# Three edits to a linear-attention and feed-forward kernel: the last tile's stores, one whole tile's store, and the grouping of batch 1's key-value products

## Chip, core and metric

The kernel runs on one core of a Trainium2 chip. The metric is the device time of one execution in microseconds; the time before is the median of three runs. All times in this document are microseconds unless marked ns.

## What is computed

The inputs are float32. Attention has no softmax: for each of 8 batches and 8 heads, with 576 positions of width 64, k and v are contracted over the positions into a 64 x 64 matrix, q is multiplied by it, and each row is divided by its root mean square and scaled. Heads are joined to rows of 512, 4608 rows in all, which go through a feed-forward layer of width 2048 with a gated activation.

```python
kv = np.einsum('bhsd,bhse->bhde', k, v)
out = np.einsum('bhsd,bhde->bhse', q, kv)
rms = np.sqrt(np.mean(out * out, axis=-1, keepdims=True) + 1e-06)
x = out / rms * g_norm                       # to (4608, 512)
h = x @ w_in                                 # (512, 2048)
g = h * (1.0 / (1.0 + np.exp(-1.702 * h)))
return (g @ w_out).astype(np.float32)        # (2048, 512)
```

## The kernel before

**Tiles.** The 4608 rows are nine tiles of 512. Tiles 0 to 7 hold 512 of the 576 positions of batches 0 to 7; tile 8 (t == B) holds the 64 positions left over of each of the eight batches. For each tile, `layers` (L758) runs the first layer (`hid_seven`, or `first_columns` for tile 0) and the second layer (`Seven.run`, L671, or `project_all`, L787, for tile 0). From tile 1 on both layers work on half-size blocks with seven products in place of eight. The attention of batch t + 1 is done in between the matmuls of tile t.

**Order of the work.** The schedule is manual: instructions stand on each engine's queue in the order in which the program makes them. `at1(i, ...)` and `at2(i, ...)` (L963, L966) put a unit of attention work behind step i of the first or second layer of the tile. Each engine takes its queue in order and waits where data is missing; SP, ACT and POOL each have a queue of DMAs besides.

**Tile 0's second layer** (`project_all`) has 64 steps, each one matmul of 128 x 512 (L795) into one of four row blocks `mo`. The steps go four output-weight blocks `fo` at a time for each `mo`; the steps from 48 on take blocks 12 and 13, then those from 52 on blocks 14 and 15. The output weights come in six loads by POOL (`load_w_out`, L195), interleaved with the loads of batch 1's q, k and v (`early_load`, L89; k and v in two halves, chunks 0 and 1, then 2 and 3). The last of these loads is that of blocks 14 and 15 (L907).

Batch 1's attention stands among these steps (L988 to L994), by chunks c of two heads: `kv(c)` (L226) makes twelve small matmuls (`early_kv_product`, L246, matmul at L250) of 96 rows and 64 columns for chunk c. After the second chunk of a pair `keep_kv` (L384) copies the pair's result to the block-diagonal weights `kvb` with two DVE copies (L387). `out(c)` (L283) multiplies q by them and squares the result on ACT (L301), `ss(c)` (L358) sums the squares with a matmul of ones and takes the root on ACT (L360), and `apply(c)` (L372) multiplies on DVE into the next tile's rows. `load_kv` (L111, POOL) for batch 2 overwrites the buffers of k and v, in two parts at steps 39 and 51; the second has DVE mask the rest rows first (`clear_rest`, L124).

**Stores.** A tile's output is gathered in `osb` (two buffers, taken in turn). `Seven.run` makes the output in quarters (i, j): i the upper or lower half of the row blocks, j the left or right half of the columns. `ORDER` (L592) makes products 1, 5, 6, 2, 7, 3, 4; `LAST` (L593), for tile 8, has 3 ahead of 7. `place` (L650) puts a quarter into `osb`: product 2 ends (0, 0), 3 ends (0, 1), 7 ends (1, 1) and 4 ends (1, 0). Every product has two halves of eight matmuls, one for each of two row blocks `mo`; in tile 8 the quarters of products 7 and 4 are placed by halves, as soon as one is done.

For tiles in `HALVED` (L953) `place` stores the upper half of the rows after quarter (0, 1) and the lower half after (1, 0), 512 KB each, on SP (`store`, L825). The other tiles from 2 to 7 are stored whole, 1 MB, behind the second layer (L774).

Tile 8 is stored by `store_rest(mo, n0, n1)` (L704): the columns n0 to n1 of one row block, which holds 64 rows of each of two batches, in two DMAs. Block 0 goes out on POOL, the others on SP and ACT, one DMA each. Blocks 0 and 1 go out at quarter (0, 1), with all 512 columns; block 3's right half at the end of (1, 1); block 2 at the first half of (1, 0); block 3's left half at the second.

Of the kernel before, what the change touches and what calls it, by code (L numbers as in the profile page):

```python
# [16 lines left out]
def kernel(  # L17
# [13 lines left out]
    DM = H * D  # L31
# [45 lines left out]
    HF, HN = FO // 2, DM // 2  # L77
# [430 lines left out]
    def copy(engine, to, src):  # L508
        (nc.vector.tensor_copy if engine == "D" else nc.scalar.copy)(to, src)  # L509
# [79 lines left out]
    class Seven:  # L589
# [60 lines left out]
        def place(self, name, mo, with_, i, j):  # L650
            ps, m = self.ready(name, mo)
            if ps is None:
                return
            o = osbs[self.t][:, 2 * i + m.start : 2 * i + m.stop, j * HN : (j + 1) * HN]
            if with_:
                nc.vector.tensor_add(o, ps, self.kept[with_][:, m])  # L656
            else:
                copy = nc.vector.tensor_copy if self.t == B else nc.scalar.copy
                copy(o, ps)
            if self.t == B:  # L660
                if (i, j) == (0, 1):
                    store_rest(0, 0, DM)
                    store_rest(1, 0, DM)
                elif i == 1 and mo == 0 and j == 0:
                    store_rest(2, 0, DM)
                elif i == 1 and mo == 1:
                    store_rest(3, j * HN, (j + 1) * HN)
            elif self.t in HALVED and j == 1 - i:
                store(self.t, 2 * i, 2 * i + 2)
# [34 lines left out]
    def store_rest(mo, n0, n1):  # L704
        osb = osbs[B]
        for g in range(2):
            rows = out[(2 * mo + g) * S : (2 * mo + g + 1) * S, n0:n1]
            if 2 * mo + g < EARLY:
                p0 = SM % PE_
                rows = rows[bass.DynSlice(NJ * p0 + SM // PE_, R, step=NJ), :]  # L710
            else:
                rows = rows[SM:S, :]
            queue = nc.gpsimd if mo == 0 else (nc.sync, nc.scalar)[g]
            queue.dma_start(out=rows, in_=osb[g * R : (g + 1) * R, mo, n0:n1])  # L714
# [43 lines left out]
    def layers(t, units1, units2):  # L758
        hid = d0 if t == 0 else Hidden(t)
        seven = Seven(t, hid.gT) if t else None  # L760
        left = hid_seven(t, hid, seven, units1) if t else first_columns(hid, units1)
        osbs[t] = opool.tile([P, 4, DM], F32, name="osb", tag="osb")
        if t:
            todo = {n: [lambda x=x: seven.sums(*x) for x in xs] for n, xs in plan(t).later.items()}
            for n, us in units2.items():
                todo.setdefault(n, []).extend(us)
            for n, us in left.items():
                todo[n] = us + todo.get(n, [])
            seven.run(todo)
        else:  # L770
            project_all(hid.gT, units2)
        if t < EARLY:
            store_early(t)
        elif t < B and t not in HALVED:  # L774
            store(t, 0, J)
# [38 lines left out]
    def store_early(t):  # L814
        n = 0
        while n < SM:
            mo, j, p = n // P, n // PE_, n % PE_
            m = min((mo + 1) * P, (j + 1) * PE_) - n
            nc.sync.dma_start(
                out=out[t * S : (t + 1) * S, :][bass.DynSlice(NJ * p + j, m, step=NJ), :],  # L820
                in_=osbs[t][n % P : n % P + m, mo, :],
            )
            n += m

    def store(t, j0, j1):  # L825
        nc.sync.dma_start(
            out=out[t * S : t * S + SM, :].rearrange("(p j) m -> p j m", j=J)[:, j0:j1],
            in_=osbs[t][:, j0:j1],
        )
# [120 lines left out]
    def plan(t):  # L950
        return SECOND if t < EARLY else LATER if t < B - 1 else LAST_TWO

    HALVED = (2, 3, 4, 5, 6)  # L953
    live = {0: a0}

    def start(b):
# [2 lines left out]
    for t in range(NT):  # L959
        b = t + 1  # L960
        u1, u2 = {}, {}

        def at1(i, f, *args):  # L963
            u1.setdefault(i, []).append(lambda: f(*args))

        def at2(i, f, *args):  # L966
            u2.setdefault(i, []).append(lambda: f(*args))  # L967

        def of(b, name, *args):
            return lambda: getattr(live[b], name)(*args)  # L970

        if t == 0:
            for l in range(2):
                at1(6, nc.vector.memset, kvd[l], 0.0)
            at1(7, of(0, "out", NPAIR))
            at1(7, scale_w_in, 0, 4)
            at1(7, w_in_sums, 0, 2)
            at1(8, start, 1)
            at1(12, scale_w_in, 4, 6)
            at1(12, w_in_sums, 2, 3)  # L980
            at1(13, load_q, 2)
            at2(4, setattr, a0, "ss_pool", Attention.ss_pool)
            at2(4, of(0, "ss", NPAIR, True))
            at2(4, of(0, "apply", NPAIR))
            at2(18, weight_sum, 0, 0, HF)
            at2(18, scale_w_in, 6, 8)
            at2(18, w_in_sums, 3, 4)
            for c in range(NPAIR):  # L988
                at1(12, of(1, "pack_q", c))
                at2(9 + 3 * c, of(1, "q", c))  # L990
                at2((36, 37, 49, 50)[c], of(1, "kv", c))
                at2((41, 43, 54, 55)[c], of(1, "out", c))
                at2((45, 50, 58, 60)[c], of(1, "ss", c))
                at2((48, 52, 58, 62)[c], of(1, "apply", c))  # L994
            for n in range(1, 4):
                at2(19, weight_sum, n, 0, 4)
                at2(38, weight_sum, n, 4, 6)
            at2(39, load_kv, 2, 0, H // 2, False)
            at2(51, clear_rest)
            at2(51, load_kv, 2, H // 2, H)  # L1000

            def first_sum():
                made[1] = Sums(1, xT[1])
                made[1].form(0)

            at2(55, first_sum)
        elif b < B:
            todo = plan(t)
            at1(todo.steps.index("kv"), of(b, "kv_all", todo.keep))
            if t == 1:  # L1010
                at1(5, start, b)
                at1(5, of(b, "transpose_q"))
                at1(4, nc.scalar.preload_act_table_set, "gelu_apprx_sigmoid_and_others")
                for n, i in ((1, 8), (2, 11), (3, 16)):
                    at1(i, weight_sum, n, 6, HF)
            if t + 2 < B:
                late = max(15, todo.steps.index("kv") + 1)
                at1(late, load_kv, t + 2)
                at1(late, load_q, t + 2)
                at2(100, start, t + 2)  # L1020
                at2(100, of(t + 2, "transpose_q"))
            at = todo.attn
            at2(at["table"], nc.scalar.preload_act_table_set, "abs_reciprocal_sqrt_and_small")
            for h in range(2):
                at2(at["roots"][h], of(b, "roots", h))
            for j in range(J):
                if j < J // 2:
                    at2(at["rows"][j], of(b, "rows", j))
                for name in ("add_up", "turn"):
                    at2(at[name][j], of(b, name, j))  # L1030
            at2(46, of(b, "out", NPAIR))
            at2(74, of(b, "ss", NPAIR))
            at2(80, of(b, "apply", NPAIR))
            at2(82, nc.scalar.preload_act_table_set, "gelu_apprx_sigmoid_and_others")
        elif t < B:
            for name in ("ss_pool", "rest_pool"):
                at2(16, setattr, live[1], name, (ps_a, "att"))
            at2(16, of(1, "out", NPAIR))
            at2(34, nc.scalar.preload_act_table_set, "abs_reciprocal_sqrt_and_small")
            at2(44, of(1, "ss", NPAIR))  # L1040
            at2(50, of(1, "apply", NPAIR))
            at2(52, nc.scalar.preload_act_table_set, "gelu_apprx_sigmoid_and_others")
        layers(t, u1, u2)
# [30 lines left out]
```

## Time and profile before

| | |
|---|---|
| median of three runs | 260.13 |
| range of the three | 260.03 to 260.14 |
| the profiled execution, its own time | 260.59 |
| its span | 258.8 |
| TensorE busy | 251.4 (97%) |
| VectorE busy | 195.1 (75%) |
| ScalarE busy | 174.9 (68%) |
| bytes moved by DMA | 35.33 MB |

The span runs from the first to the last recorded instruction; the time of an execution is longer by what lies around it, here 1.8. In the views PE is TensorE, PEld its weight loads, DVE VectorE, ACT ScalarE, POOL GpSimd and SP SyncE; a "q" behind the name marks an engine's sequencer, where DMAs are issued. L250 is line 250 of the kernel.

The page's strips cut the span into 40 slices of 6.5; a digit is the busy share in tenths. The chain that ended last is followed back from the last instruction, at each step to what released it; its rows hold start, length, and what. A row of a timeline holds start, length from the first start to the last end, engine, line, operation, tiles (out<-in), shape and count; in brackets stands the engine's idle time ahead of it and what ended it. Matmuls are pipelined: one's length is longer than the distance to the next start. A row of DMA issues holds tiles, queue, count, size of one, and the time from issue to landing. A row of windows holds the window, its length, and for each engine its busy time and count, then the granted clock, the DMA engines' busy share and their GB/s.

### The profile page before, as it was taken

How to read it: one execution, taken by the hardware profiler on the slowest of the kernel's cores; microseconds unless marked ns; L12 is line 12 of the kernel's file. 1: busy time of each engine (PE TensorE's matmuls, PEld its weight loads, DVE VectorE, ACT ScalarE, POOL GpSimd, SP SyncE). 2: the span in 40 equal slices, each digit the busy share in tenths (PEclk: the TensorE clock that was granted, in tenths of full speed). 3: DMA queues.
4: the chain of work that ended last, by engine and by line, in shares of the span. 5: the costliest groups of instructions: out<-in, count | busy, mean ns of one | idle time of the engine just before them, and what ended most of it. 6: DMA issues, size and time to landing. Idle time of an engine off the chain costs nothing.

```text
span 258.8 us, 6349 instructions
## 1 busy us (share of the span) xinstructions
PE 251.4 (97%) x2596; PEld 203.7 (79%) x2596; DVE 195.1 (75%) x351; ACT 174.9 (68%) x315; POOL 53.8 (21%) x81
## 2 busy tenths in 40 slices
PE   8889999999999999999999999999999999999993
PEld 2434454788888888888888888888888888888882
DVE  1565685899968896899689968996899687557842
ACT  3378734988749974997489748984798569737820
POOL 8773245107026001600170007000000000000001
PEclk9999999999999999999999999999999999999999
DMA  7999999999989957996799579947600610021005
GB/s 169 192 196 205 205 204 197 218 214 124 175 182 150 226 66 154 159 214 79 167 152 221 65 177 149 228 50 178 160 4 0 172 73 3 0 89 77 3 0 162
DMA packets 68559, 35.33 MB, mean 136 GB/s; under 512 B 37874, under 2 KB 65778, under 8 KB 68402
## 3 DMA queue, kind: packets, MB, share of 16 engines
q0 software_dynamic: 37520, 18.17, 54.4%
q1 hardware_dynamic: 30688, 16.36, 26.9%
q8 instruction: 20, 0.33, 0.5%
q10 hardware_dynamic: 322, 0.39, 0.4%
q14 instruction: 9, 0.07, 0.1%
HBM read 36.70 MB, written 9.44 MB: 178 GB/s over the span
## 4 chain that ended last, share of the span: by engine, by line
PE 92%; DMA 4%; DVE 1%; issue 0%; ACT 0%; POOL 0%
PE o L681 38%; PE h L559 38%; PE o L795 6%; PE hT L452 5%; DMA qraw<-in_q_dram 2%; DMA vbuf<-in_v_dram 2%; PE kvp L238 2%; PE outR L313 1%; PE ss L358 1%; PE kvp L250 0%; PE outT L283 0%; PE q L433 0%; DVE xT L368 0%; PE outT L287 0%; ACT rs L360 0%
## 5 line engine op out<-in xcount | busy, mean ns | idle before, releaser
L539 ACT ACTIVATE gT<-h 128x512 f16<-128x512 f32 x96 | 52.5, 602 | 5.4 <-PE h L559 5.4
L559 PEld LDWEIGHTS <-ws 128*128 128x128 f16 x512 | 50.1, 98 | 5.8
L681 PEld LDWEIGHTS <-gS 128*128 128x128 f16 x512 | 49.4, 98 | 6.2 <-DVE gS L611 0.3
L559 PE MATMUL h<-xS,ws 128*128 128x256 f16 x384 | 52.2, 273 | 0.0
L681 PE MATMUL o<-tw,gS 128*128 128x256 f16 x384 | 46.5, 273 | 0.0
L681 PEld LDWEIGHTS <-gT 128*128 128x128 f16 x384 | 37.6, 98 | 4.3
L559 PEld LDWEIGHTS <-w_in_sb 128*128 128x128 f16 x384 | 37.1, 98 | 4.7
L559 PE MATMUL h<-xT,w_in_sb 128*128 128x256 f16 x224 | 31.9, 273 | 0.0
L681 PE MATMUL o<-w_out_sb,gT 128*128 128x256 f16 x256 | 31.4, 273 | 0.0
L573 DVE TENSOR_TENSOR h<-h,s 128x512 f32<-128x512 f32 x32 | 22.2, 698 | 6.8 <-PE h L559 5.5
L575 DVE TENSOR_TENSOR s<-h,s 128x512 f32<-128x512 f32 x32 | 22.1, 692 | 4.1 <-PE h L559 3.3
L656 DVE TENSOR_TENSOR osb<-o,qf 128x512 f32<-128x512 f32 (+1 forms) x25 | 16.7, 668 | 11.2 <-PE o L681 8.3
L114 POOL DMA_DIRECT2D kraw<-in_k_dram x7 | 6.0, 853 | 90.6 <-PE kvp L238 86.4
L611 DVE TENSOR_TENSOR gS<-gT 128x512 f16<-128x512 f16 (+2 forms) x32 | 21.3, 686 | 0.6 <-ACT gT L539 0.6
L539 ACT ACTIVATE gT<-s 128x512 f16<-128x512 f32 x32 | 19.8, 628 | 2.6 <-DVE s L575 2.6
L714 POOL DMA_DIRECT2D out_dram<-osb x2 | 1.1, 562 | 92.0 <-DVE osb L656 92.0
L559 PE MATMUL h<-xS,w_in_sb 128*128 128x256 f16 x128 | 18.9, 273 | 0.0
L360 ACT ACTIVATE rs<-ss,eps_t 128x512 f32<-128x512 f32 (+1 forms) x16 | 9.2, 581 | 13.8 <-PE ss L358 13.7
L967 ACT ACT_TABLE_LOAD x14 | 18.0, 1283 | 0.2
L648 ACT COPY qf<-o 128x512 f32<-128x512 f32 (+1 forms) x26 | 14.2, 547 | 4.5 <-PE o L681 4.3
L329 DVE TENSOR_REDUCE sum<-sq 128x8 f32<-128x512 f16 x24 | 15.3, 678 | 2.5 <-ACT sq L323 2.5
L509 ACT COPY h<-h 128x512 f32<-128x512 f32 x27 | 15.7, 586 | 2.1 <-PE h L559 2.0
(100 smaller groups left out, 362.9 us busy)
## 6 DMA issues: line engine op xcount, KB each, us to landing
out_dram<-osb SPq DMA_DIRECT2D x10, 512.0 KB, 3.6
kraw<-in_k_dram POOLq DMA_DIRECT2D x5, 512.0 KB, 9.2
vbuf<-in_v_dram POOLq DMA_DIRECT2D x5, 512.0 KB, 12.1
qraw<-in_q_dram POOLq DMA_DIRECT2D x3, 512.0 KB, 13.2
qbuf<-in_q_dram POOLq DMA_DIRECT2D x3, 512.0 KB, 13.4
out_dram<-osb SPq DMA_DIRECT2D x6, 192.0 KB, 6.2
w_in_sb<-in_moe_w_in_dram POOLq DMA_DIRECT2D x2, 512.0 KB, 10.7
w_out_sb<-in_moe_w_out_dram POOLq DMA_DIRECT2D x2, 512.0 KB, 15.3
```

The source lines that it names most:

```text
L329: nc.vector.tensor_reduce(out=self.sum4[:, j, :], in_=self.o[j][1].rearrange("p (x d) -> p x d", d=D), op=ALU.add, axis=mybir.AxisListType.X,)
L509: (nc.vector.tensor_copy if engine == "D" else nc.scalar.copy)(to, src)
L539: nc.scalar.activation(self.gT[:, to, n * TH : (n + 1) * TH], src, AFT.Gelu_apprx_sigmoid)
L559: nc.tensor.matmul(bank[name][:, a], w, x, start=(p in (1, 5) and a == 0 and k == 0), stop=(k == KH - 1), skip_group_check=True,)
L573: nc.vector.tensor_add(bank["z"], bank["x"], self.s5)
L575: nc.vector.tensor_add(self.s5, bank["x"], self.s5)
L611: op(s[:, n, lo], a, b)
L648: nc.scalar.copy(self.kept[as_][:, m], ps)
L656: nc.vector.tensor_add(o, ps, self.kept[with_][:, m])
L681: nc.tensor.matmul(o, a, w, start=(p in (1, 2, 5) and i == 0 and (mo == 0 or split)), stop=(i == HF - 1), skip_group_check=True,)
L795: nc.tensor.matmul(os[mo], gT[:, fo, mo * P : (mo + 1) * P], w_out_sb[:, fo, :], start=(fo == 0), stop=(fo == FO - 1),)
L967: u2.setdefault(i, []).append(lambda: f(*args))
```

## The change

Three edits. When a quarter of tile 8's upper half is placed, its columns of blocks 0 and 1 are stored: (0, 0) with columns 0 to 255, (0, 1) with 256 to 511. So eight DMAs of 64 KB stand where four of 128 KB stood, half of them at the earlier quarter. Tile 6 leaves `HALVED` and is stored whole, in one DMA behind its second layer. And batch 1's `kv(1)` moves from step 37 to 36, `kv(3)` from step 50 to 49, so that 24 small matmuls follow each other at both places. Within a step, units go in the order in which the loop over c adds them: behind step 50 the `ss(1)` stays, which had stood ahead of `kv(3)` and now comes after it.

```diff
             if self.t == B:
-                if (i, j) == (0, 1):
-                    store_rest(0, 0, DM)
-                    store_rest(1, 0, DM)
+                if i == 0:
+                    for m in range(2):
+                        store_rest(m, j * HN, (j + 1) * HN)
                 elif i == 1 and mo == 0 and j == 0:
                     store_rest(2, 0, DM)
...
-    HALVED = (2, 3, 4, 5, 6)
+    HALVED = (2, 3, 4, 5)
...
-                at2((36, 37, 49, 50)[c], of(1, "kv", c))
+                at2((36, 36, 49, 49)[c], of(1, "kv", c))
```

On each engine's queue this gives: on TensorE the two groups, with nothing else moved; on POOL two more DMAs, on SP one more for tile 8 and one fewer for tile 6, on ACT one more. DVE's and ACT's operations keep their order.

## Prediction

> **What bounds the kernel now.** I read the page first, for the span and the state of the DMA engines, then the chain that ended last.
>
> ```profile
> span 258.8 us, 6349 instructions
> DMA  7999999999989957996799579947600610021005
> PE 92%; DMA 4%; DVE 1%; issue 0%; ACT 0%; POOL 0%
> ```
> ```profile
> 7.95 5.73 DMA vbuf<-in_v_dram
> 13.68 0.14 issue
> 13.81 0.38 PE kv L250 x12
> ...
> 244.02 10.60 PE o L681 x97
> ...
> 254.64 0.42 DVE osb L659
> ```
>
> TensorE carries 92% of the chain, so time taken out of its stream counts, unless something else then comes last. Two stretches are not TensorE's. In the first 45 us the DMA engines are 90% busy or more in nearly every slice; they are loading weights and the inputs of batches 0, 1 and 2. The row of 13.68 shows a landing that TensorE waits for: 0.14 us from landing to first product. The other stretch is the end. The chain closes with a DVE copy at 254.64 + 0.42 = 255.06, but the span lasts to 258.8: 3.7 us in which only stores run. The change touches both stretches, and one quiet place between them.
>
> **Part 1: batch 1's key-value products in two groups of 24.** TensorE's timeline in tile 0's second layer:
>
> ```profile
> 38.48 0.38 PE L250 MATMUL kvp<-vbuf,kraw 96*64 96x64 f16 x12
> 38.79 0.39 PE L795 MATMUL o<-w_out_sb,gT 128*128 128x512 f16 x1
> 39.11 0.38 PE L250 MATMUL kvp<-vbuf,kraw 96*64 96x64 f16 x12
> 39.42 1.04 PE L795 MATMUL o<-w_out_sb,gT 128*128 128x512 f16 x4
> 40.29 0.38 PE L283 MATMUL outT<-qT,kvb 128*128 128x512 f16 x1
> ...
> 42.76 0.38 PE L250 MATMUL kvp<-vbuf,kraw 96*64 96x64 f16 x12
> 43.07 0.39 PE L795 MATMUL o<-w_out_sb,gT 128*128 128x512 f16 x1
> 43.30 0.38 PE L358 MATMUL ss<-sq,ones 128*128 128x512 f16 x1
> 43.60 0.38 PE L250 MATMUL kvp<-vbuf,kraw 96*64 96x64 f16 x12
> 43.91 1.04 PE L795 MATMUL o<-w_out_sb,gT 128*128 128x512 f16 x4
> ```
>
> Matmuls overlap, so I go by starts. Four L795 take 40.29 - 39.42 = 0.87, or 0.22 each. The single one between two key-value groups takes 39.11 - 38.79 = 0.32, so entering a group costs 0.10. Twelve products take 38.79 - 38.48 = 0.31. What 24 take isn't in the trace; the nearest row is a later tile's group of 40:
>
> ```profile
> 57.06 0.82 PE L238 MATMUL kvp<-vbuf,kraw 128*64 128x64 f16 x40
> 57.81 0.61 PE L559 MATMUL h<-xT,w_in_sb 128*128 128x256 f16 x4
> ```
>
> Forty take 0.75, so one more product costs (0.75 - 0.31) / 28 = 0.016, and 24 take 0.31 + 12 x 0.016 = 0.50 where two groups took 0.62. A merge saves 0.12 + 0.10 = 0.22, and both 0.44. That is the upper bound.
>
> The groups and steps also wait for loads, all on POOL's queue: the third and fourth product for the second half of batch 1's v (issued at 30.57), and step 52 of the layer, the first to use output-weight blocks 14 and 15, for the last weight load (issued at 33.10). These are the issues, and for each the size and the time to landing:
>
> ```profile
> 30.57 0.68 POOL L90 DMA_DIRECT2D vbuf<-in_v_dram  x1 [1.91 <-DMA qraw<-in_q_dram]
> 33.10 0.70 POOL L196 DMA_DIRECT2D w_out_sb<-in_moe_w_out_dram  x1 [1.85 <-DMA w_out_sb<-in_moe_w_out_dram]
> ```
> ```profile
> vbuf<-in_v_dram POOLq DMA_DIRECT2D x1, 288.0 KB, 12.0
> ```
> ```profile
> w_out_sb<-in_moe_w_out_dram POOLq DMA_DIRECT2D x1, 256.0 KB, 10.7
> ```
>
> They land at 42.57 and 43.80. Nothing ahead of them in the queue is changed, so they land then after the change too. With the 0.14 of the first fence, the third product can't start before 42.71 and step 52 not before 43.94. The first merge would bring the third product from 42.76 to 42.54: the load holds it at 42.71. From there 24 products (0.50), step 50, the sum of squares, and step 51 (0.22 each) bring step 52 to 43.87: the weights hold it at 43.94. In the trace it starts at 43.91 + 0.22 = 44.13. So 0.19 us is left of 0.44, and what is late next is the weight load. Below, the part is bounded by 0 (the step might be at its load already); I take **0.2**.
>
> The copies of the products to the weights of the next step cost nothing:
>
> ```profile
> 39.53 0.59 DVE L387 CAST kvb<-kvp 64x128 f16<-64x128 f32 x2 [0.70 <-PE kvp L250]
> ```
>
> They begin 0.11 behind the start of the step that follows the group. After the change that step starts at 38.48 + 0.50 = 38.98, the copies end at 39.68, and the product that reads them comes five steps on, at 40.08; the slack grows from 0.17 to 0.40. In the second group it is six matmuls instead of four. The sum of squares of chunk 1 now stands behind the fourth product, at 43.43 instead of 43.30, and its apply is due three steps later, behind the mask of the rest rows on DVE, which itself comes earlier. POOL's loads for batch 2, which wait for these products, are issued up to 0.4 earlier, behind the weights in the same queue.
>
> **Part 2: tile 6 in one transfer.** SP issues the second half of the tile's store at 206.12, and that half takes 2.6 us to land; the whole now goes out at that point:
>
> ```profile
> 206.12 0.33 SPq L826 DMA_DIRECT2D out_dram<-osb  x1
> ```
> ```profile
> out_dram<-osb SPq DMA_DIRECT2D x1, 512.0 KB, 2.6
> ```
>
> At twice the half's time it lands at 211.3. Nothing stands behind it on SP before tile 7's own store, tile 8 first writes the same buffer at 249.46 (fence of part 3), and the DMA engines have little to do in those slices (the page's row). Cost and gain: 0. If that cover were gone, the wait would be for one half more, 2.6.
>
> **Part 3: the last tile's upper left quarter.** DVE makes the upper left quarter at 249.46 and the upper right one at 251.22; the stores of both follow at 251.94 on SP and ACT, at 252.21 on POOL:
>
> ```profile
> 249.46 0.69 DVE L656 TENSOR_TENSOR osb<-o,qf 128x512 f32<-128x512 f32 x1 [2.63 <-issue]
> 251.22 1.23 DVE L656 TENSOR_TENSOR osb<-o,qf 128x512 f32<-128x512 f32 x2 [1.07 <-PE o L681]
> ...
> 251.94 3.62 SPq L714 DMA_DIRECT2D out_dram<-osb  x4
> 252.21 1.11 POOL L714 DMA_DIRECT2D out_dram<-osb  x2 [91.99 <-DVE osb L656]
> ```
>
> What the DMA engines do in each microsecond behind that (the last two columns are their busy share and GB/s), and the size and time to landing of the last two transfers:
>
> ```profile
> 252.00:253.00 1.00, 1.00 (x11) 0.90 (x10) 0.53 (x2) 0.00 (x0) 0.80 (x2) 1.00 0.00 0
> 253.00:254.00 1.00, 1.00 (x11) 0.90 (x10) 0.55 (x2) 0.00 (x0) 0.32 (x1) 1.00 0.89 188
> 254.00:255.00 1.00, 0.61 (x6) 0.29 (x3) 0.55 (x2) 0.00 (x0) 0.00 (x0) 1.00 0.87 256
> 255.00:256.00 1.00, 0.00 (x0) 0.00 (x0) 0.07 (x1) 0.00 (x0) 0.00 (x0) 1.00 0.85 269
> 256.00:257.00 1.00, 0.00 (x0) 0.00 (x0) 0.00 (x0) 0.00 (x0) 0.00 (x0) 1.00 0.86 289
> 257.00:258.00 1.00, 0.00 (x0) 0.00 (x0) 0.00 (x0) 0.00 (x0) 0.00 (x0) 1.00 0.14 46
> ```
> ```profile
> out_dram<-osb SPq DMA_DIRECT2D x1, 64.0 KB, 2.5
> out_dram<-osb ACTq DMA_DIRECT2D x1, 64.0 KB, 2.7
> ```
>
> The whole last tile, 1 MB, moves from 253.0 (1.1 us behind the first issue) to about 257.2, without a pause: the end is a queue that is full until the last transfer. The last, issued at 255.1, behind the last copy, lands at 257.8, 0.6 behind its last bytes; 1.0 more closes the span. The stores before it are issued at 254.2 and 253.35: the steps are half products of eight matmuls, 0.87 each (10.60 / 97 x 8). The change sends 256 KB from 250.15 on, moved by about 252.3 while the engines are idle. At 0.27 MB/us (the rows of 254 to 257) the rest goes so: 256 KB from 253.0 to 254.0; 128 KB from 254.45 to 254.95; 256 KB from 255.3 to 256.3; the last 128 KB to 256.8. Landing 257.35 instead of 257.8: a gain of **0.45**. Upper bound: with nothing ahead of it, 1.1 + 128 KB at that rate (0.5) + 0.6 = 2.2 against 2.7, with the rounding 0.6. Lower bound 0, below. Four more issues (one on SP, one on ACT, two on POOL) stand ahead of the others, when SP, ACT and POOL have nothing else; behind them wait only the later stores, whose data comes 1.8 us later.
>
> The Trainium skill speaks against this part: "DMA: Bandwidth & Descriptors", section "Rules for kernel authors", says to coalesce many small transfers, since below 64 KB one pays mostly overhead, and the upper quarters now go in eight transfers of just 64 KB. By the fit in the same page's "Anatomy of one DMA", 2.0 us and the bytes at 436 GB/s, the last 64 KB would land 2.15 after issue, an estimate that would make the gain 0.55 instead of 0.45. No row here shows a lone transfer of that size.
>
> **Sum.** 0.2 + 0 + 0.45 = 0.65 off the profiled execution's 260.59 (258.8 and 1.8 around it): 259.94. The median of the runs shown is 260.13, 0.46 lower, so **259.5**. From no change a measurement tells about 0.2%, 0.5 us; the forecast is just beyond it.
>
> **Rivals.**
> *The tail keeps its length.* If each transfer costs a fixed time in the queue and not its bytes, ten in 4.2 us are 0.42 each, and ten still stand behind 251.94; the four new ones would be through by 251.3 + 1.7 = 253.0, and cost nothing. Gain 0, time 260.13 - 0.2 = 259.9. This is where the Trainium skill's rule on coalescing ("DMA: Bandwidth & Descriptors") leads. For it: 64 KB take nearly as long to land (2.5) as 512 KB in the quiet at 206.12 (2.6). Against: a rate that rises to 289 GB/s and a busy share of 0.85 or more until the last bytes.
> *No load holds part 1.* If the loads land 0.25 earlier than in the profiled execution, the full 0.44 comes: 260.13 - 0.89 = 259.2.
> *Slower: POOL's closing drain.* POOL now makes four stores at the end instead of two, and it closes with a drain of 4.7 us:
>
> ```profile
> L1069 POOLq DRAIN  x3: 51/102/4737, 252.7 to 258.5; - x3
> ```
>
> It runs from 252.7 to 257.4, 4.1 behind the end of POOL's last issue at 253.3. If it goes by the number of POOL's transfers, it takes 2.05 for each, and would end at 253.3 + 8.2 = 261.5; with 1.0 to close, the span would end at 262.5, less part 1's 0.2: 3.5 more, 263.6. It decides as soon as the drain outlasts the last landing, 257.35. Against it: it ends within 0.2 of the last bytes of all queues, which looks like a wait for traffic, and then it gets shorter too.
>
> **Chances and range.** Forecast 0.55 (0.05 of it within 0.2%), no gain in the tail 0.26, no load in the way 0.12, drain 0.07. So faster by over 0.2% 0.62, within it 0.31, slower 0.07. The bounds of the parts, 0 to 0.44 and 0 to 0.6, give 259.1 to 260.1; I take 259.0 to 260.1 and leave the drain out.
>
> **What would show it.** Two rows of L250 x24, each 0.50 to the next start, and one L795 less between them. Step 52 0.2 earlier, with the last weights' landing just ahead of it, and every later row of TensorE up to the last copy (254.4) early by as much. DMA busy from 251 to 252.4, then a hole, and gaps between the later stores; the last transfer landing 2.2 to 2.3 behind its issue; span 258.15. The forecast falls if the last landing stays at 2.7 behind its issue, if loads land later than they did, or if POOL's drain ends behind the last landing.

## The result, and the profile after

| | before | after |
|---|---|---|
| median of 15 runs each | 260.14 | 259.32 |
| lowest to highest | 259.86 to 262.07 | 258.98 to 259.98 |
| the profiled execution, its own time | 260.59 | 259.37 |
| its span | 258.8 | 257.6 |

The ratio is 0.9966, with a 95% interval of 0.9953 to 0.998: the change makes the kernel 0.8 to 0.9 us faster. The forecast of 259.5 was 0.2 too high; direction and range were right. A second set of runs of the changed kernel (below) gave a smaller gain, 0.9984 (0.9972 to 0.9996); the two intervals overlap.

The page of the changed kernel, the rows that answer to those of before:

```profile
span 257.6 us, 6353 instructions
DMA  7999999999989947996799479948600430012005
PE 92%; POOL 3%; DMA 3%; issue 0%; DVE 0%
```

TensorE still carries 92% of the chain. Not all of the 1.2 us between the two spans is the change's: the first key-value product of tile 0's second layer starts at 38.01 instead of 38.48, and ahead of it no edit has done anything yet. Batch 0's last key-value product, which the chain of before waits for at 13.81, starts at 12.74 here, behind an earlier landing of v. So 0.47 of the pair's difference is chance, and distances behind that first product are what can be compared.

**TensorE around the two merged groups**, the changed kernel's timeline:

```profile
38.01 0.57 PE L250 MATMUL kvp<-vbuf,kraw 96*64 96x64 f16 x24
38.51 1.25 PE L795 MATMUL o<-w_out_sb,gT 128*128 128x512 f16 x5
39.60 0.38 PE L283 MATMUL outT<-qT,kvb 128*128 128x512 f16 x1
...
41.11 1.03 PE L795 MATMUL o<-w_out_sb,gT 128*128 128x512 f16 x4
42.07 0.57 PE L250 MATMUL kvp<-vbuf,kraw 96*64 96x64 f16 x24
42.57 0.39 PE L795 MATMUL o<-w_out_sb,gT 128*128 128x512 f16 x1
42.80 0.38 PE L358 MATMUL ss<-sq,ones 128*128 128x512 f16 x1
43.01 1.03 PE L795 MATMUL o<-w_out_sb,gT 128*128 128x512 f16 x4
43.87 0.38 PE L283 MATMUL outT<-qT,kvb 128*128 128x512 f16 x1
```

A group of 24 takes 38.51 - 38.01 = 0.50, and the group and its five steps 39.60 - 38.01 = 1.59, where before they took 40.29 - 38.48 = 1.81. That is the 0.22 of the prediction, and the second merge brings 0.23 more: from the first product to the product with q at 43.87 it is 5.86, against 6.31 before. The last weight load is this one:

```profile
32.06 0.70 POOL L196 DMA_DIRECT2D w_out_sb<-in_moe_w_out_dram  x1 [1.86 <-DMA w_out_sb<-in_moe_w_out_dram]
```
```profile
w_out_sb<-in_moe_w_out_dram POOLq DMA_DIRECT2D x1, 256.0 KB, 10.7
```

It lands at 42.8, and step 52, the second of the four L795 behind 43.01, starts at 43.23. So no load held this execution, and it kept the full 0.45.

**The tail.** DVE's last copy, the DMA issues of the last pair (size and time to landing), and POOL's drain, of the changed kernel:

```profile
253.72 0.42 DVE L659 COPY osb<-o 128x256 f32<-128x256 f32 x1 [0.45 <-PE o L681]
```
```profile
out_dram<-osb SPq DMA_DIRECT2D x1, 64.0 KB, 2.3
out_dram<-osb ACTq DMA_DIRECT2D x1, 64.0 KB, 2.4
```
```profile
L1069 POOLq DRAIN  x3: 51/102/3432, 251.7 to 257.3; - x3
```

The copy ends at 254.14 and the last landing follows at 256.61, 2.47 behind it (before 2.71); the span's end stands 3.45 behind the copy (before 3.75). POOL's drain became shorter with its four transfers, 3.43 us instead of 4.74, and ends at 255.1, 1.5 ahead of the last landing of all. In both profiles it ends 1.1 behind POOL's own last landing (253.98 here, 256.33 before). The windows of the tail (last two columns: DMA busy share, GB/s):

```profile
251.00:252.00 1.00, 1.00 (x12) 0.89 (x11) 0.45 (x2) 0.00 (x0) 0.72 (x2) 1.00 0.46 148
252.00:253.00 1.00, 1.00 (x12) 0.90 (x10) 0.55 (x2) 0.00 (x0) 0.33 (x1) 1.00 0.70 163
253.00:254.00 1.00, 0.69 (x7) 0.37 (x4) 0.55 (x2) 0.00 (x0) 0.00 (x0) 1.00 0.68 193
254.00:255.00 1.00, 0.00 (x0) 0.00 (x0) 0.15 (x1) 0.00 (x0) 0.00 (x0) 1.00 0.72 153
255.00:256.00 1.00, 0.00 (x0) 0.00 (x0) 0.00 (x0) 0.00 (x0) 0.00 (x0) 1.00 0.79 266
```

Before, the engines were idle until 253.0 and then 0.85 to 0.89 busy. Now they begin early, and none of these windows shows more than 0.79. Yet the last pair lands only 0.2 to 0.3 sooner behind its issue (2.3 and 2.4, where it was 2.5 and 2.7).

### The profile page after: what moved, and what is told of

It reads as the page before. It is cut to its first block, busy times and chain, and to the rows that moved or that the text cites. A ratio compares the mean times of both kernels' runs of the same rounds, so it can differ in the third digit from the quotient of the medians.

```text
span 257.6 us, 6353 instructions
## 1 busy us (share of the span) xinstructions
PE 250.6 (97%) x2596; PEld 203.3 (79%) x2596; DVE 195.0 (76%) x351; ACT 174.9 (68%) x315; POOL 55.0 (21%) x83
## 4 chain that ended last, share of the span: by engine, by line
PE 92%; POOL 3%; DMA 3%; issue 0%; DVE 0%
PE o L681 38%; PE h L559 38%; PE o L795 5%; PE hT L452 5%; DMA w_in_sb<-in_moe_w_in_dram 3%; PE kvp L238 2%; PE outR L313 1%; POOL kraw L90 1%; POOL qraw L90 1%; PE ss L358 1%; POOL vbuf L90 1%; POOL w_in_sb L171 0%; PE q L433 0%; PE kvp L250 0%; PE outT L283 0%; PE outT L287 0%
## 5 line engine op out<-in xcount | busy, mean ns | idle before, releaser
L681 PE MATMUL o<-tw,gS 128*128 128x256 f16 x384 | 46.5, 273 | 0.0
L714 POOL DMA_DIRECT2D out_dram<-osb x4 | 2.2, 546 | 90.9 <-DVE osb L656 90.9
L559 PE MATMUL h<-xS,w_in_sb 128*128 128x256 f16 x128 | 18.9, 273 | 0.0
## 6 DMA issues: line engine op xcount, KB each, us to landing
qraw<-in_q_dram POOLq DMA_DIRECT2D x3, 512.0 KB, 13.4
w_in_sb<-in_moe_w_in_dram POOLq DMA_DIRECT2D x2, 512.0 KB, 10.7
```

The source lines that it names most:

```text
L559: nc.tensor.matmul(bank[name][:, a], w, x, start=(p in (1, 5) and a == 0 and k == 0), stop=(k == KH - 1), skip_group_check=True,)
L681: nc.tensor.matmul(o, a, w, start=(p in (1, 2, 5) and i == 0 and (mo == 0 or split)), stop=(i == HF - 1), skip_group_check=True,)
```

## Experiments

Ratios are against the kernel before, on the same chip: e1 to e4 share their runs of it (median 260.37), and e6, e9, e10 and the repeat of the change theirs (260.20); e11 ran on another chip, where the median was 260.20 too; beside e5, e7 and e8 one execution of it took 260.27. A ratio is not quite the quotient of two medians: for e2 it stands for 0.55 us, the medians are 0.32 apart.

My theory: part 1 is worth 0.44 less what loads hold back, part 3 drains a backlog of bytes. Rivals: the tail pays for starts and not for bytes; and the merges gain nothing.

**The parts alone.** Kernel e1 is before with edit 3 only, e2 with the merges only, e3 with tile 6 only; e4 cuts the upper quarters in half but writes all four stores at the later quarter.

```diff
 # e1
+                if i == 0:
+                    for m in range(2):
+                        store_rest(m, j * HN, (j + 1) * HN)
 # e2
+                at2((36, 36, 49, 49)[c], of(1, "kv", c))
 # e3
+    HALVED = (2, 3, 4, 5)
 # e4
                 if (i, j) == (0, 1):
+                    for h in range(2):
+                        for m in range(2):
+                            store_rest(m, h * HN, (h + 1) * HN)
```

> The last tile's stores alone. By the prediction's theory (the end is a full queue of bytes) the last landing comes 2.2 to 2.3 behind its issue instead of 2.7, and the time falls by 0.45. By the theory from the two traces (the last pair on SP and ACT pays its own start, ACT's behind SP's, and only the part that waits for bytes goes) the landing stays at 2.4 to 2.5 and the time falls by 0.2 to 0.3. If splitting costs a fixed time for each transfer, the time is unchanged or longer. TensorE's steps stay as before in all three.

> The two groups of 24 alone. By the prediction's theory the loads hold the second group's step 52, and 0.2 is left of 0.44. By the theory from the two traces each merge gives 0.22 from the first product to the step that reads the result, and both count (0.44) in executions in which the last weight load lands at least 0.2 ahead of step 52; the load holds it only in an execution whose loads run late. The end behind TensorE stays as before: last landing 2.7 behind its issue.

> Tile 6 in one transfer alone. By both theories no change: the transfer lands before 212 and nothing waits for it before 249. If it did count, the time would move by more than 0.3 either way. It shows besides how far two executions of the same work differ in their first 15 us.

> The kernel before, with the last tile's upper quarters in eight transfers of 64 KB, but all of them at the second quarter, where four of 128 KB stood: the split without the earlier start. If the end is bound by bytes, the time is unchanged (within 0.1). If each transfer costs a fixed time in the queue, four more at 0.42 make it longer by up to 1.7; if only the two more on SP and ACT count, by 0.3 to 0.8, with the last landing 3.0 or more behind its issue.

| | median | ratio (95%) | last copy to last landing, to span end | L250's first product to the product with q |
|---|---|---|---|---|
| e1 | 260.01 | 0.9991 (0.9976 to 1.0007) | 2.56, 3.74 | 6.32 |
| e2 | 260.05 | 0.9979 (0.9958 to 1.0) | 2.80, 3.85 | 5.87 |
| e3 | 260.60 | 1.0009 (0.9993 to 1.0025) | 2.75, 3.85 | 6.31 |
| e4 | 260.04 | 0.9986 (0.9968 to 1.0003) | 2.38, 3.56 | 6.31 |

By times alone only e2's interval comes near to excluding no change, 0.55 us less in the middle; the traces tell more. The merges give 0.45 on TensorE and nothing in the tail; edit 3 shortens the landing by 0.15 in e1 and leaves TensorE as it is, and the span's end is no earlier there (3.74 behind the copy, 3.75 before); edit 2 alone does nothing. e1's last transfer lands 2.5 behind its issue: not the 2.2 to 2.3 of the full queue of bytes, nor the 2.7 of no gain.

The 0.45 stays to the end of TensorE's work. From the first product of the first group to the end of the last copy it is 216.6 in all five profiles without the merges in which no load is late (before, e1, e3, e4, e10), and 216.1 in five with them (the change, e2, e5, e6, e9).

e2's profiled execution nonetheless took 261.23. Its timeline, and the windows of e2 and of e1 (third column from the right: granted clock):

```profile
39.43 0.57 PE L250 MATMUL kvp<-vbuf,kraw 96*64 96x64 f16 x24
...
45.30 0.38 PE L283 MATMUL outT<-qT,kvb 128*128 128x512 f16 x1
```
```profile
13.00:15.00 2.00, 1.75 (x16) 0.97 (x17) 1.02 (x4) 0.69 (x1) 1.82 (x3) 0.61 1.22 183
15.00:17.00 2.00, 2.00 (x7) 0.68 (x6) 0.72 (x1) 0.60 (x1) 1.36 (x3) 0.54 1.40 180
```
```profile
13.00:15.00 2.00, 1.92 (x20) 1.02 (x21) 1.26 (x3) 1.09 (x2) 1.83 (x3) 1.00 1.30 208
```

Its first product is at 39.43, later than in any other profile but e4's (39.67). Both executions had about 3.4 us at half the clock from 13.4 on, long before the edits' place. That is chance, and it is why the spans aren't compared here.

e4 didn't test what it was made for. Its program writes all stores at the later quarter, but each of SP's stores waits only for its own data:

```profile
250.66 0.69 DVE L656 TENSOR_TENSOR osb<-o,qf 128x512 f32<-128x512 f32 x1 [2.64 <-issue]
252.42 1.23 DVE L656 TENSOR_TENSOR osb<-o,qf 128x512 f32<-128x512 f32 x2 [1.07 <-PE o L682]
```
```profile
251.38 5.39 SPq L715 DMA_DIRECT2D out_dram<-osb  x5
```

SP issues the first left half at 251.38, 0.03 behind its sum, as the change does. So e4 is e1 once more, and its ratio agrees with e1's. Its last landing, 2.38 behind the copy where e1's is 2.56, shows how far two executions of the same tail differ.

**What the last landing waits for.** From the changed kernel, e5 doesn't store the upper quarters at all; e6 leaves out ACT's half of the very last pair. From the kernel before, e10 is what e4 was to be: the halves in the order right, left, so that all wait for the later quarter.

```diff
 # e5
                 if i == 0:
+                    pass
-                    for m in range(2):
-                        store_rest(m, j * HN, (j + 1) * HN)
 # e6, in store_rest
+                if (mo, n0, g) == (3, 0, 1):
+                    continue
 # e10
                 if (i, j) == (0, 1):
+                    for h in (1, 0):
+                        for m in range(2):
+                            store_rest(m, h * HN, (h + 1) * HN)
```

> The changed kernel without the stores of the last tile's blocks 0 and 1 (the upper quarters are not stored). If what is left of the end is block 2's and 3's own stores and fixed times, the last landing stays at 2.4 to 2.5 behind its issue, as in the changed kernel. If the upper quarter's bytes still stand in its way, it falls to 2.2 or less.

> The changed kernel without the very last transfer, that of ACT (half of block 3's left columns is not stored): SP's last then has nothing beside it. If the last pair's two transfers go through one after the other, SP's lands 2.0 to 2.3 behind its issue, as it does now (2.29), and the span ends 0.15 to 0.4 earlier than with both. If they share the engines' bytes, SP's own landing also comes earlier, by 0.2 or more.

> The kernel before, with the upper quarters in eight transfers of 64 KB, the right columns queued first, so that the left ones can't go out before the second quarter is done: the split without the earlier start, which the run with the left columns first did not give. If the end is bound by bytes, the last landing stays at 2.7 to 2.8 behind its issue. If a transfer costs a fixed time on SP's and ACT's queue, two more there make it 3.1 to 3.6.

One execution of e5 took 259.22, with a span of 257.5. Its last copy, and its last two DMAs:

```profile
253.28 0.42 DVE L659 COPY osb<-o 128x256 f32<-128x256 f32 x1 [0.45 <-PE o L680]
```
```profile
out_dram<-osb SPq DMA_DIRECT2D x1, 64.0 KB, 2.3
out_dram<-osb ACTq DMA_DIRECT2D x1, 64.0 KB, 2.5
```

With half the bytes of the tile gone, the last landing is 2.52 behind the last copy, no sooner than with them (2.47). So what edit 3 leaves of the upper quarters' bytes costs nothing that can be seen, and there was about 0.2 to gain from them (2.71 less 2.52, one execution each).

One execution of e6 took 258.79, with a span of 257.0. SP's lone transfer lands sooner, 2.15 behind the last copy:

```profile
out_dram<-osb SPq DMA_DIRECT2D x1, 64.0 KB, 2.1
```

So 0.3 of the rest goes with its partner on ACT: 0.15 because ACT's landing, the later of the two, is gone, and 0.17 because SP's own comes sooner, 2.12 behind its issue instead of 2.29. That lies between the two cases of the expectation (2.0 to 2.3 if the two go one after the other, 0.2 or more sooner if they share), and SP's in the repeat, with its partner, took 2.19; so e6 doesn't decide between them. In the changed kernel the first packets of SP's transfers start 1.1 to 1.3 behind the issue, those of ACT's, issued at the same time, 1.4 to 1.8. Even the first pair, which found the engines idle at 249.26, takes this:

```profile
out_dram<-osb SPq DMA_DIRECT2D x1, 64.0 KB, 2.0
out_dram<-osb ACTq DMA_DIRECT2D x1, 64.0 KB, 2.8
```

e10: 260.44, ratio 1.0018 (1.0004 to 1.0031). The last landing is 2.67 behind the last copy, as before (2.71), although two transfers more stand ahead of it on SP and ACT. A fixed price for each transfer in the queue isn't there; the earlier start is what helps. By the ratio e10 is 0.47 us slower, by the medians 0.24. Its tail's end accounts for 0.12 (3.87 against 3.75), all of it behind the landing. The rest shows in no part of its trace, and stays open.

**Do loads hold the merges?** Here the last weight load is put behind batch 2's q in POOL's queue, in the kernel before (e8) and with the merges (e7).

```diff
 # e8; e7 has the merges as well
-    (the call of load_w_out for blocks 14 and 15)
...
+    at1(13, load_w_out, 14, FO)
```

> The two groups of 24 alone, with the last weight load moved behind batch 2's q load, so that it lands about 2.6 later. The prediction's rule is that step 52 starts at the later of the stream and the landing + 0.14. Here the landing holds it, so from the landing to step 52 there are 0.1 to 0.15, TensorE stands for 1.5 to 2.5, and the two merges bring nothing to the time of step 52. If the merges counted whatever the loads do, step 52 would still come 0.44 earlier than in the same kernel without them, measured from the first load's landing.

> The kernel before with the same late weight load. Step 52 again 0.1 to 0.15 behind the landing, at the same distance from the loads' start as with the groups of 24; if the merges counted regardless, 0.44 later.

Measured, one execution each: e7 264.36, span 262.6; e8 264.91, span 263.1. The chains of e7 and of e8:

```profile
37.02 9.35 DMA w_out_sb<-in_moe_w_out_dram
46.38 0.04 issue
46.42 1.44 PE o L795 x3
```
```profile
37.14 9.77 DMA w_out_sb<-in_moe_w_out_dram
46.91 0.04 issue
46.95 1.31 PE o L795 x3
```

Both wait for the load, e7 2.3 and e8 2.0 us. From that landing to the last copy's end it is 212.45 in e7 and 212.47 in e8: where the load holds, the merges are worth nothing. The spans differ by what the landings do, 0.5. Their issues, ahead of the merges in POOL's queue, are already 0.12 apart; that the rest is chance too is not shown, with one execution each. From landing to matmul are 0.04, where the expectation had 0.1 to 0.15.

**The repeat, and block 2 in halves.** The changed kernel once more; e9 stores block 2 of the last tile in two halves; e11 adds to e9 that tiles 4 and 5 are stored whole, which removes two DMAs of SP far ahead of the end.

```diff
 # e9
-                elif i == 1 and mo == 0 and j == 0:
-                    store_rest(2, 0, DM)
+                elif i == 1 and mo == 0:
+                    store_rest(2, j * HN, (j + 1) * HN)
 # e11: e9 and
+    HALVED = (2, 3)
```

> The changed kernel once more, beside the one with block 2 in halves and on the same chip. From the first product of the first group to the last product with q, 5.86 as before the repeat and 6.31 in the kernel before; last landing 2.4 to 2.5 behind its issue; the time 0.5 to 0.9 below the kernel before.

> The changed kernel, with block 2 of the last tile stored in halves too: its right columns at the first half of quarter (1, 1), its left ones at the first half of (1, 0), so that four pairs of 64 KB go out 0.87 apart on SP and ACT. If the last pair waits for the bytes of block 2 ahead of it, it starts 1.1 to 1.4 behind its issue and lands 2.2 behind it instead of 2.4 to 2.5, as the changed kernel's pair of block 3's right half does: 0.25 less than the changed kernel, so 0.9 to 1.0 less than before. If it is two fixed starts and no waiting, the landing stays at 2.4 to 2.5 and the time is the changed kernel's. If each transfer costs a fixed time, two more make it longer.

> The changed kernel with block 2 in halves, and tiles 4 and 5 stored whole as well: two DMAs fewer on SP, so that the last pair of stores uses the last two of the eight completion semaphores instead of the first two. The kernel's end waits for the eight in a fixed order, one after the other at about 0.06 each. If that order counts, the end of the span comes 3.1 to 3.25 behind the last copy, against 3.57 with block 2 in halves alone, 3.4 in the changed kernel and 3.8 before, and the time is 1.0 to 1.1 below the kernel before. If the order is no matter, the end stays at 3.5 to 3.6 behind the last copy. If storing tiles 4 and 5 whole delays the loads of the tiles behind them, TensorE's steps between 100 and 210 get longer.

| | median | ratio (95%) | last copy to last landing, to span end |
|---|---|---|---|
| change, repeated | 259.62 | 0.9984 (0.9972 to 0.9996) | 2.39, 3.37 |
| e9 | 259.68 | 0.9981 (0.9972 to 0.9989) | 2.22, 3.57 |
| e11 | 259.58 | 0.9983 (0.997 to 0.9997) | 2.23, 3.22 |

The times miss what was expected of them: e9 is 0.5 us below the kernel before, not 0.9 to 1.0, e11 0.4 by the ratio and 0.6 by the medians, not 1.0 to 1.1, and the repeat 0.4 and 0.6, where 0.5 to 0.9 stood. The tails of e9 and e11 came as expected.

*The landing.* With 64 KB instead of 128 KB ahead of it, the last pair lands 0.15 to 0.25 sooner than in the changed kernel (2.39 and 2.47). So block 2's bytes still stood in its way there. *The close.* e9 loses that again behind the landing. SP's last instructions wait for the eight completion semaphores, which the DMAs of SP and ACT take in turn, always in the same order. Of e9 and e11, SP's waits from the last landing on (count, shortest/median/longest in ns, first and last start):

```profile
L1069 SPq EVENT_SEMAPHORE  x10: 17/28/28, 256.6 to 257.9; - x10
```
```profile
L1069 SPq EVENT_SEMAPHORE  x4: 17/22/28, 257.2 to 258.1; - x4
```

In e9 the last pair used one of the first semaphores that are asked for, and the others' waits, some 0.06 each, stand behind the landing; in e11 it used the last. The landing is the same in both, the span ends 0.35 sooner. The times of e9 and e11 don't show this difference. The changed kernel and e1 differ in the same way, by tile 6's one DMA:

```profile
L1069 SPq EVENT_SEMAPHORE  x4: 17/22/28, 256.6 to 257.5; - x4
```
```profile
L1069 SPq EVENT_SEMAPHORE  x10: 17/28/28, 256.7 to 258.0; - x10
```

From landing to span's end it is 0.98 in the changed kernel and its repeat, 1.18 in e1 and e4, and 1.04 before, with five waits.

*Another gate.* The repeat's timeline:

```profile
37.61 0.57 PE L250 MATMUL kvp<-vbuf,kraw 96*64 96x64 f16 x24
...
41.78 0.57 PE L250 MATMUL kvp<-vbuf,kraw 96*64 96x64 f16 x24
...
43.61 0.38 PE L283 MATMUL outT<-qT,kvb 128*128 128x512 f16 x1
...
55.87 0.32 PE L238 MATMUL kvp<-vbuf,kraw 128*64 128x64 f16 x8
56.59 0.69 PE L238 MATMUL kvp<-vbuf,kraw 128*64 128x64 f16 x32 [0.40 <-DMA vbuf<-in_v_dram]
```
```profile
45.87 0.69 POOL L119 DMA_DIRECT2D vbuf<-in_v_dram  x1 [1.25 <-DMA qraw<-in_q_dram]
```
```profile
vbuf<-in_v_dram POOLq DMA_DIRECT2D x1, 64.0 KB, 10.7
```

From first product to the product with q it is 6.00: up to here this execution kept 0.31 of the 0.45. Batch 1's v landed at 41.64, 0.14 ahead of the second group, and the last weights at 42.92, 0.05 ahead of step 52. And 12 us later TensorE waits 0.40 for a load that the prediction doesn't name, the rest rows of batch 2's v, which lands at 45.87 + 10.7 = 56.57. The same group in the changed kernel's first profile, and in e11's:

```profile
56.13 0.82 PE L238 MATMUL kvp<-vbuf,kraw 128*64 128x64 f16 x40
```
```profile
56.21 0.32 PE L238 MATMUL kvp<-vbuf,kraw 128*64 128x64 f16 x8
57.03 0.69 PE L238 MATMUL kvp<-vbuf,kraw 128*64 128x64 f16 x32 [0.51 <-DMA vbuf<-in_v_dram]
```

The wait costs more than the merges gain. From this group's start to the end of the last copy it is 198.0 in the changed kernel and in the one before, 198.6 in the repeat and 198.7 in e11. So from the first product of batch 1 to the last copy these two executions took 216.9 and 216.8, more than the 216.6 of the kernel before. Behind the group, e11's work takes no longer than the changed kernel's.

In the changed kernel's first profile the load landed at 55.7, 0.4 ahead of the group; before, at 56.1 against a group at 57.06, 1.0 ahead. The merges bring the group forward, and the landing stays. Leaving out e2 and e4, it comes 17.3 to 17.7 behind the first product of batch 1 in all four profiles without the merges (before, e1, e3, e10) and in four with them (the change, e5, e6, e9), 18.9 in the repeat and e11. Why it came later in these two is open.

## Why the forecast was right, and where it was not

**Part 1, forecast 0.2, measured 0.45 to the product with q in six profiles (the change, e2, e5, e6, e9, e11), 0.31 in the repeat.** The price of a merge was right to the hundredth: 24 products from the rows of twelve and of forty, and the entry of a group at 0.10. That TensorE's chain carries it to the end is right too, where nothing else is late (216.1 against 216.6). The mis-sized term is what the loads hold back. The step "they land then after the change too" took the landing of one execution for fixed, 43.80, the latest of all the profiles in which this load keeps its place (42.5 to 43.6 in the others), and put 0.14 behind it where e7 and e8 show 0.04. (Behind v's landing the 0.14 holds, as the repeat's second group shows.) The mechanism itself is as told: the repeat was held at both places named, and e7 and e8 show that nothing is left when the load holds. So "no load holds part 1", with a chance of 0.12, was the state of six of the seven profiles with the merges and the loads in their place, and landings are to be given as a spread.

The prediction also lacked a gate: "POOL's loads for batch 2 are issued up to 0.4 earlier" treated the rest rows of v as covered. Their slack was 1.0 in the trace of before and 0.4 in that of the change, and it was gone in the repeat and in e11, which stood idle for 0.40 and 0.51 and came out 0.6 and 0.7 later. What the merges gain is then more than given back, 12 us on. That such a wait lies behind the smaller gain of the second set of runs is not shown: only one execution of each set has a trace.

**Part 2, forecast 0.** Alone it is 0: e3 is at 1.0009 and its tail ends like before. "Cost and gain: 0" failed in another way. One DMA fewer turns the order of the completion semaphores, and together with edit 3 this decides whether the close takes 1.18 (e1) or 0.98 us (the change). So a part that the prediction hid behind quiet DMA engines is worth 0.2 at the end by the traces; no time shows it alone. At tile 6 itself all went as told, and better: the whole tile landed 3.9 behind its issue at 205.2, not 5.2.

**Part 3, forecast 0.45, measured 0.24 and 0.32 to the landing (the change and its repeat), 0.15 and 0.33 in e1 and e4; to the span's end 0.30 and 0.38 in the change and its repeat, part 2's share included.** The direction and the hole in the backlog are right. What failed is the step "the end is a queue that is full until the last transfer", with 0.27 MB/us for the rest. The windows of after, from 252 to 256, show 153 to 266 GB/s where it had 270, at a busy share of 0.68 to 0.79. Most of a pair's time is then its start, SP's 1.1 to 1.3 and then ACT's. e5 shows no byte of the upper quarters left in it; what is left ahead of the last pair is block 2, worth the 0.15 to 0.25 by which e9 and e11 land sooner. The 2.2 to 2.3 expected for the last transfer were 2.4; e9 and e11, with block 2 in halves, reach 2.2.

The Trainium skill's fit ("DMA: Bandwidth & Descriptors", "Anatomy of one DMA"), which the page gives for DMAs that GpSimd issues, would have 2.15 for 64 KB, an estimate. The prediction used it for the last pair, which goes out on SP and ACT. POOL's own 64 KB stores took 2.2 to 2.3 in the changed kernel, near to it, and SP's lone transfer in e6 2.1; the last pair took 2.3 and 2.4, and there the measurement decides. The same page's rule to coalesce spoke for the rival that "the tail keeps its length". The change's tail is 0.3 shorter with more and smaller transfers, and e10, with the same number and no earlier start, stays at 2.67: here it is the start that counts, not their number.

**The rivals.** The tail doesn't keep its length. POOL's drain doesn't go by the number of its transfers: with four it took 3.43, not 8.2. But the reason given against that rival was wrong: the drain doesn't follow "the last bytes of all queues", which end 1.0 behind it in the changed kernel (256.1 and 255.1). It ends 1.1 behind POOL's own last landing, and this comes earlier because its data came earlier.

**The sum.** The forecast's 0.2 + 0 + 0.45 stood for two things: 0.45, less a wait in some executions, and 0.3 to 0.4 in the tail, with part 2's share inside. The total came out near, 0.63 from the median against 0.82 measured. That is in part luck: part 1 was taken too small and part 3 too large.

## What to carry to other kernels

Price a merge on the engine that carries the chain from the starts of its neighbours; then follow every load in the next ten microseconds, and hold its slack against the spread of landings over several profiles. At the end of a kernel, start stores as soon as their data exist, and keep those just ahead of the last one small; most of what is left is the last one's start, and here that of a second transfer issued beside it. Look also at what closes the program: a DMA removed 50 us ahead changed the close by 0.2 us.

## What was not expected of the hardware

*The closing waits.* SP's row of ten waits against four is 0.35 us in e9 and e11, from the order of completion semaphores alone.

*Pairs start one after the other.* Of two 64 KB stores issued together on SP and ACT into idle DMA engines, SP's landed 2.0 and ACT's 2.8 behind the issue; leaving out ACT's at the end (e6) brought the last landing from 2.47 to 2.15 behind the copy. Whether ACT's start is late because of SP's or is so by itself is open: no run leaves SP's out.

*Half a clock for 3.4 us.* The profiles of e2 and e4 hold one stretch at a granted clock of 0.5 from 13.4 or 13.5 to 16.9, and their first key-value product of batch 1 is at 39.4 and 39.7, where all others have it between 37.6 and 39.1; in e7 and e8 the clock drops in the same way at 46.5 and 47.1, around the end of TensorE's wait of 2 us. The Trainium skill, "TensorE: Matmul & The Clock Gate", "Part 1: The HAM clock gate", has the clock decided in windows of some 3.4 us, at half the rate after an idle one; the length and the 0.5 agree. The idle window doesn't: in e2 TensorE was busy for 2.5 of the 3.4 us from 10.0 to 13.4, and the changed kernel, with 2.7 of the same stretch, kept its full clock. What sets the half clock off in e2 and e4 stays open. That such stretches make up much of the scatter between single runs, up to 262 us for the kernel before, is a guess: runs without a trace don't show it.
